# Converting double-precision weights beside attention: from three-step pieces to a pipeline over slots

## The chip, the cores and the metric

The kernel runs on one core of a Trainium2 chip. The core has five engines with a queue of instructions each: TensorE (PE, with its weight loads as PEld), VectorE (DVE), ScalarE (ACT), GpSimd (POOL) and SyncE (SP), which here only issues DMAs. Each engine runs its queue in program order, and semaphores join the queues. The metric is the device time of one launch in microseconds; the profile comes from one separate profiled execution.

## What is computed

The reference first runs an attention with a threshold over 8 batches, 8 heads, 576 tokens and a head dimension of 64, in float32. A score that lies more than tau below its row's maximum is dropped before the softmax. The 8 heads of a token are joined to 512 features, and a mixer follows:

```python
scores = scale * np.matmul(q, k.transpose(0, 1, 3, 2))
thresh = np.max(scores, axis=-1, keepdims=True) - tau
scores = np.where(scores >= thresh, scores, -1000000000.0)
attn = softmax(scores); x = heads_joined(np.matmul(attn, v))
h = np.maximum(xt @ w_tok1, 0.0) @ w_tok2      # xt: features x tokens
u = x + h.transpose(0, 2, 1)
out = u + np.maximum(u @ w_ch1, 0.0) @ w_ch2
```

The four weights (576x256, 256x576, 512x1536, 1536x512) arrive as 64-bit floats. The kernel turns them into 32-bit floats itself, with integer and float operations on the two 32-bit words of each number.

## The kernel before

**Attention.** The work goes in 144 units, 18 per batch; a unit is 128 query rows of two heads. In the main loop (from L513) a unit does its scores on TensorE (`scores`, L286), the row maxima on VectorE (L291) and a small bias on GpSimd (L292). Then `weigh` puts the threshold (L301) and the exponential (L304) on ScalarE. One unit later `norm` divides by the row sum (reciprocal on VectorE, L310 and L311; scaling on GpSimd, L314). Two units later the weights are transposed. In batch 0 TensorE does it and VectorE or ScalarE copies the result (`turn`, L337 and L339). In later batches VectorE transposes blocks (`turn_blocks`, L348), and 16 DMAs on SP's queue move the blocks (L358), for every second unit and for the shared one. `values` multiplies with v (L388, L393) and ScalarE copies to xT (L398). The scores lie in PSUM in two double-bank buffers, three in batch 0, so new scores wait until ScalarE has read the old ones at L301.

**MLP.** When a batch's attention is complete, `push` puts its mixer steps into a list: transposes of x (L412, L413), the token products (L422, L429, with VectorE adding the result to xT at L433), and the channel products (L451 with ScalarE's ReLU at L452; L463 and L467 with the copy at L472 and a DMA out). `fill` takes steps from the list in three portions of each unit, 0.4, 0.3 and 0.3 of a quota worked out from written costs. So TensorE's order is the program's, and batch 0 has no MLP steps. They begin in unit 20, once batch 0 is complete. The products share two PSUM buffers.

**Weights.** There are 31 pieces: three of w_tok1, four of w_tok2 (288 columns), 12 of w_ch1, 12 of w_ch2, most of 128 x 512 numbers. `load_piece` (L187, its DMA on SP at L196) brings a piece into one of three raw buffers in a scratch tile. `f64_to_f32` (L145) has six instructions:

- ScalarE L159: the low words, scaled by 2^-29, in place
- ScalarE L160: the square of the high words read as floats, into the one buffer h2
- VectorE L161 and L164: shift and mask the exponent's and the fraction's bits, into one of two buffers a; put the sign back
- VectorE L167: zero for numbers that are too small, by h2
- GpSimd L168: the integer add of a and the low words, into the weight tile

The generator yields after L161, after L164, and after L168 with the load of the piece three further on. One yield is a step, so three steps make a piece. `weight(n)` (L216) takes n steps at two places in the loop: at L544, before `weigh`, and at L556, at the end of the unit. n is 1 and 1 in batch 0, then 4 and 3. `need(i)` (L224) takes the steps that piece i still lacks before a matmul reads it.

Of the kernel before, what the change touches and what calls it, by code (L numbers as in the profile page):

```python
# [9 lines left out]
F32 = mybir.dt.float32  # L10
U32 = mybir.dt.uint32
I32 = mybir.dt.int32
I64 = mybir.dt.int64
AF = mybir.ActivationFunctionType
ALU = mybir.AluOpType
AX = mybir.AxisListType

P = 128
# [3 lines left out]
def kernel(  # L22
# [26 lines left out]
    nc = tc.nc  # L49
# [21 lines left out]
    work = ctx.enter_context(tc.tile_pool(name="work", bufs=2))  # L71
# [38 lines left out]
    def load_v(n):  # L110

        b, p = pairs[n]
        lv = ld.tile([P, NK, D], F32, tag="lv", bufs=4, name=f"lv_{n}")
        nc.sync.dma_start(out=lv, in_=v[b].rearrange("h s d -> (h s) d")[2 * S * p : 2 * S * p + 2 * S, :].rearrange("(c p) d -> p c d", p=P))
        vals[n] = lv
# [15 lines left out]

    WMAX = 512
    scratch = work.tile([P, NP * 2 * S], U32, tag="xT", name="scratch")
    NRAW = 3
    raw_at = [scratch[:, 2 * WMAX * i : 2 * WMAX * (i + 1)] for i in range(NRAW)]
    a_at = [scratch[:, 2 * WMAX * NRAW + WMAX * i : 2 * WMAX * NRAW + WMAX * (i + 1)] for i in range(2)]
    sq_at = scratch[:, 2 * WMAX * NRAW + 2 * WMAX : 2 * WMAX * NRAW + 3 * WMAX].bitcast(F32)
    turn_of = [0]

    def like(x, dst):  # L140
        if len(dst.shape) == 2:
            return x
        return x.rearrange("p (a b) -> p a b", a=dst.shape[1])

    def f64_to_f32(dst, raw, rows, n):  # L145

        lo, hi = raw[:, :, 0], raw[:, :, 1]
        a = a_at[turn_of[0] % 2][0:rows, 0:n]
        h2 = sq_at[0:rows, 0:n]
        turn_of[0] += 1
        af = a.bitcast(F32)
        nc.scalar.activation(out=lo.bitcast(I32), in_=lo, func=AF.Copy, scale=2.0**-29)  # L159
        nc.scalar.activation(out=h2, in_=hi.bitcast(F32), func=AF.Square)  # L160
        yield nc.vector.tensor_scalar(  # L161
            out=a, in0=hi, scalar1=3, scalar2=0x3FFFFFFF, op0=ALU.logical_shift_left, op1=ALU.bitwise_and
        )
        yield nc.vector.scalar_tensor_tensor(  # L164
            out=a, in0=hi, scalar=0xC0000000, in1=a, op0=ALU.bitwise_and, op1=ALU.bitwise_or
        )
        nc.vector.scalar_tensor_tensor(out=af, in0=h2, scalar=2.0**-30, in1=af, op0=ALU.is_ge, op1=ALU.mult)  # L167
        nc.gpsimd.tensor_tensor(  # L168
            out=dst.bitcast(I32), in0=like(a.bitcast(I32), dst), in1=like(lo.bitcast(I32), dst), op=ALU.add
        )  # L170

    pieces = [
        (w1[:, 2 * i : 2 * i + 2, :], moe_w_tok1[2 * P * i : 2 * P * i + 2 * P, :].rearrange("(t p) x -> p t x", p=P))
        for i in range(NI // 2)
    ]
# [6 lines left out]
    for j in range(NJ):  # L182
        pieces.append((wc2[:, j, :], moe_w_ch2[P * j : P * j + P, :]))

    raws = {}

    def load_piece(i):  # L187
        dst, src = pieces[i]
        rows = dst.shape[0]
        n = 1  # L190
        for d in dst.shape[1:]:
            n *= d
        wide = src.dtype == I64
        raw = raw_at[i % NRAW][0:rows, 0 : n * (2 if wide else 1)]
        raw = raw.bitcast(src.dtype)
        nc.sync.dma_start(out=like(raw, dst), in_=src)  # L196
        raws[i] = raw, rows, n

    def weight_ops():
        for i, (dst, src) in enumerate(pieces):  # L200
            raw, rows, n = raws.pop(i)
            if src.dtype == I64:
                for _ in f64_to_f32(dst, raw.bitcast(U32).rearrange("p (n w) -> p n w", w=2), rows, n):
                    yield
            else:
                yield
                yield
                nc.gpsimd.tensor_copy(out=dst, in_=like(raw, dst))
            if i + NRAW < len(pieces):
                load_piece(i + NRAW)  # L210
            yield

    wops = weight_ops()
    steps_done = 0

    def weight(n):  # L216

        nonlocal steps_done
        for _ in range(n):
            if next(wops, wops) is wops:  # L220
                return
            steps_done += 1

    def need(i):  # L224

        weight(3 * i + 3 - steps_done)

    load_piece(0)
    load_qk(1, (nc.sync, nc.sync))
# [1 line left out]
    for i in range(1, NRAW):  # L231
        load_piece(i)
    load_v(1)

# [23 lines left out]
    def in_blocks(b):  # L260
        return b > 0
# [10 lines left out]
    def scores(u):  # L272
        b, p0, t = units[u]
        sc = [
            (ps_3rd if b == 0 and (2 * u + h) % 3 == 2 else ps_sc).tile([P, 2, MAIN], F32, tag="sc", name=f"sc{h}_{u}") for h in range(2)
        ]
        if t == SHARED:
            parts = [(b * NP + p0 + i, slice(MAIN, S), slice(64 * i, 64 * i + 64)) for i in range(2)]
        else:
            i, c = divmod(t - (t > SHARED), NI)  # L280
            parts = [(b * NP + p0 + i, slice(P * c, P * c + P), slice(0, P))]
        order = [(f, part, h) for f in range(2) for part in parts for h in range(2)]
        for f, (n, cols, rows), h in order if b else sorted(order, key=lambda o: o[2]):
            r = slice(D * h, D * h + D)
            qT, kT = heads[n]
            nc.tensor.matmul(sc[h][rows, f, 0:HS], lhsT=qT[r, cols], rhs=kT[r, HS * f : HS * f + HS], start=True, stop=True)  # L286
        mx = small.tile([P, 2], F32, tag="mx", name=f"mx_{u}")
        bias = small.tile([P, 2], F32, tag="bias", name=f"bias_{u}")
        for h in range(2):
            c = slice(h, h + 1)  # L290
            nc.vector.tensor_reduce(out=mx[:, c], in_=sc[h][:, :, 0:HS], axis=AX.XY, op=ALU.max)  # L291
            nc.gpsimd.tensor_scalar(out=bias[:, c], in0=mx[:, c], scalar1=toff, scalar2=-SCALE, op0=ALU.add, op1=ALU.mult)  # L292
        st[u] = sc, bias
# [13 lines left out]
    def norm(u):  # L307
        e, rs = st[u]
        rr = small.tile([P, 2], F32, tag="rr", name=f"rr_{u}")
        nc.vector.tensor_scalar(out=rr, in0=rs, scalar1=1e-9, scalar2=None, op0=ALU.add)  # L310
        nc.vector.reciprocal(out=rr, in_=rr)  # L311
        for h in range(2):
            eh = e[:, S * h : S * h + S]
            nc.gpsimd.tensor_scalar(out=eh, in0=eh, scalar1=rr[:, h : h + 1], scalar2=1.0, op0=ALU.mult, op1=ALU.mult)  # L314
        st[u] = e
# [195 lines left out]
    b_now = 0  # L511
    LAG = 2
    for u in range(len(units) + LAG + 4):  # L513
        on = u < len(units)
        if u == UB:
            late.close()
            ps_mm = ctx.enter_context(tc.tile_pool(name="ps_mm", bufs=2, space=bass.MemoryType.PSUM))
        if on:
            b_now, p0, t = units[u]
            n = b_now * NP + p0  # L520
        w = u - LAG
        back = 0 <= w < len(units)
        if on:
            scores(u)
        if 0 < u <= len(units):
            norm(u - 1)
        if back:
            key, place, many = group_of(w)
            if in_blocks(key[0]):
                turn_blocks(w)  # L530
            else:
                for i in range(3):
                    turn(w, i)
            if place == many - 1:
                b, p, c = key
                if c == 0 and p % 2 == 0:
                    split_middle(b * NP + p)
                if c == "s":
                    split_middle(b * NP + p + 1)
                when = u + (2 if in_blocks(b) else 1)  # L540
                due += [(when, b, p + i, c) for i in range(2 if c == "s" else 1)]
        if b_now:
            fill(0.4)
        weight(4 if b_now else 1)  # L544
        if on:
            weigh(u)
        if b_now:
            fill(0.3)
        while due and due[0][0] <= u:
            _, b, p, c = due.popleft()  # L550
            values(b, p, c)
            if p == NP - 1 and c == 1:
                push(b)
        if b_now:
            fill(0.3)
        weight(3 if b_now else 1)  # L556
        if on:
            m = n + 2 + t // 4
            if t < 8 and m < len(pairs):
                load_qk(m, (nc.scalar if b_now else nc.sync,) * 2, t % 4)  # L560
                if t % 4 == 3:
                    load_v(m)
            if t == 2:
                prep(n + 1)
            if t == 7 and n + 2 < len(pairs):
                prep(n + 2)
    weight(10000)
    quota = 1e9
    fill(1.0)
# [28 lines left out]
```

## Time and profile before

| | |
|---|---|
| median of three runs | 1420.17 us (1418.49 to 1422.05) |
| profiled execution | 1421.9 us span, 1424.03 us device time, mean granted TensorE clock 0.984 |
| TensorE busy | 1346.7 us, 95% |
| its weight loads | 832.4 us, 59% |
| VectorE busy | 584.1 us, 41% |
| ScalarE busy | 589.8 us, 41% |
| GpSimd busy | 345.4 us, 24% |
| first and last L168 | 18.9 us, 201.1 us |

The shares are means over the whole span. The page's slices cut the span into 40 parts of 35.5 us, with a digit for each engine's busy tenths and a line for the clock that TensorE was granted. The windows view gives busy time for any stretch. The waits view says in one line which instruction stood idle, what released it, how long in total, how often, and the longest. The groups view lists instructions of one kind: busy time, mean ns of one, then the idle time before them and what ended it. The timeline lists instructions in order: start, length, queue, line. The chain of waits goes back from the last instruction to what released each step.

### The profile page before, as it was taken

Reading aid. Unit: us, or ns where it says so; the run is one execution under the profiler, and the core shown is the slowest. Engines: PE = TensorE matmul, PEld = TensorE weight load, DVE = VectorE, ACT = ScalarE, POOL = GpSimd, SP = SyncE. Lnnn points to the kernel's source line nnn. Section 1 sums busy time; section 2 is a strip of 40 time slices with the busy share of each in tenths; the row PEclk is TensorE's granted clock in tenths of the full one; section 3 lists DMA queues with packets and bytes.
Section 4 is the critical chain, followed back from the end, with each engine's and each line's share of the span. In section 5 each row is a group of like instructions: output and inputs, shape, how many; then the busy total and the mean of one; then the engine's idle time right before and its main releaser. Section 6 shows DMA issues by size and latency. Waiting matters only on the chain.

```text
span 1421.9 us, 19495 instructions
## 1 busy us (share of the span) xinstructions
PE 1346.7 (95%) x6866; PEld 832.4 (59%) x6866; DVE 584.1 (41%) x1009; ACT 589.8 (41%) x1328; POOL 345.4 (24%) x681
## 2 busy tenths in 40 slices
PE   6777689988999999999999999999999999999998
PEld 4443455645656566565656566566657466566675
DVE  5888654344344443434433444334333443201000
ACT  5776353443545444353434444353334344220110
POOL 4565332222222222222212222222121222100000
PEclk9998899989999999999999999999999999999999
DMA  6344544443444434443343534443433433300000
GB/s 130 90 117 131 152 125 103 92 116 84 102 120 111 108 84 106 104 98 80 92 101 77 121 80 111 104 98 69 103 87 83 111 91 78 82 15 15 8 8 23
DMA packets 257376, 128.34 MB, mean 90 GB/s; under 512 B 208064, under 2 KB 221376, under 8 KB 257280
## 3 DMA queue, kind: packets, MB, share of 16 engines
q1 hardware_dynamic: 131632, 111.46, 29.9%
q10 hardware_dynamic: 125648, 15.64, 6.9%
q8 instruction: 55, 0.90, 0.3%
q14 instruction: 41, 0.34, 0.1%
HBM read 43.25 MB, written 9.44 MB: 37 GB/s over the span
## 4 chain that ended last, share of the span: by engine, by line
PE 81%; DVE 8%; SPq 5%; DMA 3%; ACT 3%; issue 1%; POOL 0%; DVEq 0%; ACTq 0%
PE c L467 26%; PE c L451 24%; PE sc L286 10%; PE pv L393 7%; SPq L358 5%; PE t L422 3%; PE t L429 3%; DVE mx L291 3%; PE pv L388 2%; DVE T L348 2%; PE tx L412 2%; PE c L463 1%; DMA eT<-T 1%; DMA scratch<-in_moe_w_ch_dram 1%; ACT e L301 1%
## 5 line engine op out<-in xcount | busy, mean ns | idle before, releaser
L451 PE MATMUL c<-xT,wc 128*128 128x256 f32 (+1 forms) x1920 | 406.2, 363 | 1.9 <-DVE xT L433 0.8
L291 DVE TENSOR_REDUCE mx<-sc 128x1 f32<-128x576 f32 x288 | 204.6, 751 | 489.5 <-PE sc L286 489.4
L467 PE MATMUL c<-wc,g 128*128 128x512 f32 x864 | 389.5, 597 | 0.0
L451 PEld LDWEIGHTS c<-xT,wc 128*128 128x128 f32 x1920 | 331.7, 190 | 75.9 <-issue 29.9
L292 POOL TENSOR_SCALAR bias<-mx,toff 128x1 f32<-128x1 f32 x288 | 76.7, 267 | 807.8 <-DVE mx L291 754.1
L301 ACT ACTIVATE e<-sc,bias 128x576 f32<-128x576 f32 x288 | 199.2, 741 | 169.7 <-POOL bias L292 148.8
L467 PEld LDWEIGHTS c<-wc,g 128*128 128x128 f32 x864 | 157.6, 190 | 177.3 <-issue 175.9
L452 ACT ACTIVATE g<-c 128x256 f32<-128x256 f32 (+1 forms) x240 | 87.3, 364 | 386.0 <-PE c L451 366.5
L304 ACT ACTIVATE e<-e,ntau 128x576 f32<-128x576 f32 x288 | 220.8, 774 | 0.0
L314 POOL TENSOR_SCALAR e<-e,rr 128x576 f32<-128x576 f32 x288 | 213.4, 753 | 17.3 <-DVE rr L311 4.1
L286 PE MATMUL sc<-kT,qT 64*128 64x288 f32 (+1 forms) x1280 | 196.7, 441 | 20.0 <-ACT e L301 10.9
L348 DVE STREAM_TRANSPOSE T<-e 128x1152 f32<-128x1152 f32 x126 | 172.5, 1369 | 16.5 <-DMA eT<-T 10.8
L286 PEld LDWEIGHTS sc<-kT,qT 64*128 64x128 f32 (+1 forms) x1280 | 107.1, 181 | 102.1 <-issue 50.1
L393 PE MATMUL pv<-eT,lv 128*64 128x256 f32 x1024 | 124.0, 385 | 0.0
L472 DVE COPY o<-c 128x512 f32<-128x512 f32 x36 | 24.6, 684 | 192.7 <-PE c L467 192.7
L393 PEld LDWEIGHTS pv<-eT,lv 128*64 128x64 f32 x1024 | 75.7, 140 | 38.0 <-issue 2.6
L429 PE MATMUL t<-w,a 128*128 128x288 f32 x256 | 78.8, 437 | 17.8 <-DVE xT L433 15.8
L422 PE MATMUL t<-x,w 128*128 128x512 f32 (+1 forms) x160 | 76.0, 613 | 0.0
L429 PEld LDWEIGHTS t<-w,a 128*128 128x128 f32 x256 | 46.7, 197 | 42.6 <-DVE xT L433 20.8
L398 ACT COPY xT<-pv 128x256 f32<-128x256 f32 x64 | 23.9, 373 | 107.4 <-PE pv L393 107.3
L433 DVE TENSOR_TENSOR xT<-xT,t 128x288 f32<-128x288 f32 x64 | 27.9, 442 | 96.5 <-PE t L429 96.4
L304 ACT ACTIVATION_READ_ACCUMULATOR e<-e,ntau 128x1 f32 x288 | 57.4, 199 | 0.0
(43 smaller groups left out, 600.4 us busy)
## 6 DMA issues: line engine op xcount, KB each, us to landing
eT<-T SPq DMA_DIRECT2D x896, 72.0 KB, 2.0
scratch<-in_moe_w_ch_dram SPq DMA_DIRECT2D x24, 512.0 KB, 3.8
lv<-in_v_dram SPq DMA_DIRECT2D x32, 288.0 KB, 3.3
out_dram<-o SPq DMA_DIRECT2D x36, 256.0 KB, 2.2
eT<-T SPq DMA_DIRECT2D x224, 36.0 KB, 1.9
lk<-in_k_dram ACTq DMA_DIRECT2D x108, 72.0 KB, 2.7
lq<-in_q_dram ACTq DMA_DIRECT2D x104, 72.0 KB, 2.1
lq<-in_q_dram SPq DMA_DIRECT2D x24, 72.0 KB, 3.3
```

The source lines that it names most:

```text
L286: nc.tensor.matmul(sc[h][rows, f, 0:HS], lhsT=qT[r, cols], rhs=kT[r, HS * f : HS * f + HS], start=True, stop=True)
L291: nc.vector.tensor_reduce(out=mx[:, c], in_=sc[h][:, :, 0:HS], axis=AX.XY, op=ALU.max)
L301: nc.scalar.activation(out=eh, in_=sc[h][:, :, 0:HS], func=AF.Prelu, bias=bias[:, h : h + 1], scale=SCALE, alpha=STEEP)
L304: nc.scalar.activation(out=eh, in_=eh, func=AF.Exp, bias=ntau, accum_out=rs[:, h : h + 1])
L314: nc.gpsimd.tensor_scalar(out=eh, in0=eh, scalar1=rr[:, h : h + 1], scalar2=1.0, op0=ALU.mult, op1=ALU.mult)
L348: nc.vector.transpose(out=T.rearrange("p (a c n x) -> p c a n x", a=4, c=NK, n=n)[:, :, :, place, :], in_=e.rearrange("p (c a x) -> p c a ...
L393: nc.tensor.matmul(to[r], lhsT=lv[:, j, :], rhs=eT[:, j], start=False, stop=(c == NI - 1), skip_group_check=True)
L422: nc.tensor.matmul(ps, lhsT=w1[0:M, t, P * m : P * m + P], rhs=s["x"][0:M, t, :], start=(t == 0), stop=(t == NT - 1))
L429: nc.tensor.matmul(ps, lhsT=s["a"][:, m, P * c : P * c + P], rhs=w2[:, m, HS * f : HS * f + HS], start=(m == 0), stop=(m == NTK - 1))
L451: nc.tensor.matmul(ps, lhsT=wc1[:, j, c, :], rhs=uT[:, c, GR * i : GR * i + n], start=(c == 0), stop=(c == NCC - 1))
L452: nc.scalar.activation(out=s["g"][:, j, 0:n], in_=ps, func=AF.Relu)
L467: nc.tensor.matmul(flat, lhsT=s["g"][:, j, P * t : P * t + P], rhs=wc2[:, j, :], start=False, stop=(j == NJ - 1), skip_group_check=True)
```

## The change

The generator of steps is replaced by a counter of slots. In one slot GpSimd adds the piece of the slot before, ScalarE does its two operations for the piece of the slot after, VectorE does its three for the slot's own piece in a row, and the load of the piece three further than the slot's is issued on SP behind GpSimd's add. VectorE writes into the weight tile itself, and GpSimd adds in place. The raw buffers become four. The square h2 takes the two buffers of the output tile (tag "o"). ScalarE's part of piece 0 comes ahead of the main loop.

The places move too. In batch 0 there is one slot at the end of each unit but every fourth (u % 4 = 3). In later batches there is one slot right after `norm`, ahead of `turn_blocks` and its DMAs, and one at the end of the unit. `need(i)` takes slots until slot i + 1 is done.

```diff
-    NRAW = 3
+    NRAW = 4
...
+            h2 = work.tile([P, WMAX], F32, tag="o", name=f"h2_{i}")[0:rows, 0:n]
...
+    def on_scalar(i):
+        if i < len(pieces) and pieces[i][1].dtype == I64:
+            lo, hi, h2 = raws[i]
+            nc.scalar.activation(out=lo.bitcast(I32), in_=lo, func=AF.Copy, scale=2.0**-29)
+            nc.scalar.activation(out=h2, in_=hi.bitcast(F32), func=AF.Square)
...
+    def on_vector(i):
...
+            nc.vector.tensor_scalar(
+                out=bits, in0=hi, scalar1=3, scalar2=0x3FFFFFFF, op0=ALU.logical_shift_left, op1=ALU.bitwise_and
+            )
+            nc.vector.scalar_tensor_tensor(
+                out=bits, in0=hi, scalar=0xC0000000, in1=bits, op0=ALU.bitwise_and, op1=ALU.bitwise_or
+            )
+            nc.vector.scalar_tensor_tensor(out=dst, in0=h2, scalar=2.0**-30, in1=dst, op0=ALU.is_ge, op1=ALU.mult)
...
+    def weight():
+        nonlocal slot
+        if slot <= len(pieces):
+            on_gpsimd(slot - 1)
+            on_scalar(slot + 1)
+            on_vector(slot)
+            if slot:
+                load_piece(slot - 1 + NRAW)
+            slot += 1
...
     def need(i):
...
-        weight(3 * i + 3 - steps_done)
+        while slot < i + 2:
+            weight()
...
+    on_scalar(0)
...
             norm(u - 1)
+        if b_now:
+            weight()
         if back:
...
-        weight(4 if b_now else 1)
         if on:
             weigh(u)
...
-        weight(3 if b_now else 1)
+        if b_now or u % 4 < 3:
+            weight()
```

More of the change, by code (lines that the diff above doesn't have):

```diff
@@ L133 @@
     scratch = work.tile([P, NP * 2 * S], U32, tag="xT", name="scratch")
-    NRAW = 3
+    NRAW = 4
     raw_at = [scratch[:, 2 * WMAX * i : 2 * WMAX * (i + 1)] for i in range(NRAW)]
-    a_at = [scratch[:, 2 * WMAX * NRAW + WMAX * i : 2 * WMAX * NRAW + WMAX * (i + 1)] for i in range(2)]
-    sq_at = scratch[:, 2 * WMAX * NRAW + 2 * WMAX : 2 * WMAX * NRAW + 3 * WMAX].bitcast(F32)
-    turn_of = [0]
     def like(x, dst):
@@ L143, in like @@
         return x.rearrange("p (a b) -> p a b", a=dst.shape[1])
[L145 to L170, printed above, removed]
     pieces = [
@@ L187, in load_piece @@
     def load_piece(i):
+        if i >= len(pieces):
+            return
         dst, src = pieces[i]
@@ L193, in load_piece @@
         wide = src.dtype == I64
-        raw = raw_at[i % NRAW][0:rows, 0 : n * (2 if wide else 1)]
-        raw = raw.bitcast(src.dtype)
+        raw = raw_at[i % NRAW][0:rows, 0 : n * (2 if wide else 1)].bitcast(src.dtype)
         nc.sync.dma_start(out=like(raw, dst), in_=src)
[L197 to L201, printed above, removed]
+        if wide:
+            words = raw.bitcast(U32).rearrange("p (n w) -> p n w", w=2)
+            h2 = work.tile([P, WMAX], F32, tag="o", name=f"h2_{i}")[0:rows, 0:n]
+            raws[i] = like(words[:, :, 0], dst), like(words[:, :, 1], dst), like(h2, dst)
+        else:
+            raws[i] = like(raw, dst)
@@ new lines, in on_scalar @@
+    def on_scalar(i):
[4 more added lines that the diff above has]
+    def on_vector(i):
+        if i < len(pieces) and pieces[i][1].dtype == I64:
+            dst = pieces[i][0]
+            lo, hi, h2 = raws[i]
+            bits = dst.bitcast(U32)
+            nc.vector.tensor_scalar(
[5 more added lines that the diff above has]
+            nc.vector.scalar_tensor_tensor(out=dst, in0=h2, scalar=2.0**-30, in1=dst, op0=ALU.is_ge, op1=ALU.mult)
@@ L202, in weight_ops, with on_gpsimd @@
+    def on_gpsimd(i):
+        if 0 <= i < len(pieces):
+            dst, src = pieces[i]
             if src.dtype == I64:
-                for _ in f64_to_f32(dst, raw.bitcast(U32).rearrange("p (n w) -> p n w", w=2), rows, n):
-                    yield
-            else:
[L206 to L222, printed above, removed]
+                nc.gpsimd.tensor_tensor(out=dst.bitcast(I32), in0=dst.bitcast(I32), in1=raws.pop(i)[0].bitcast(I32), op=ALU.add)
+            else:
+                nc.gpsimd.tensor_copy(out=dst, in_=raws.pop(i))
+    slot = 0
+    def weight():
[7 more added lines that the diff above has]
+            slot += 1
@@ L566 @@
                 prep(n + 2)
-    weight(10000)
+    need(len(pieces) - 1)
     quota = 1e9
```

## The prediction

> **What bounds it now.** I read first the page's slices, then busy time by stage, then TensorE's waits in the stage with holes. The slices (each 35.5 us):
>
> ```profile
> PE   6777689988999999999999999999999999999998
> DVE  5888654344344443434433444334333443201000
> ...
> PEclk9998899989999999999999999999999999999999
> ```
>
> TensorE has holes in the first six slices and small ones near the ninth. Later it is full: the kernel is bound by TensorE, except where the weights are converted. The scores' start times in the timeline give the unit borders: unit 3 starts at 21.75 us, 18 (batch 1) at 98.18, 20 at 115.44, 27 at 205.86. Busy time by these stages:
>
> ```profile
> 21.75:98.18 76.43, 59.30 (x472) 38.22 (x471) 62.44 (x135) 58.08 (x128) 44.29 (x77) 1.00 0.42 97
> 98.18:115.44 17.26, 10.13 (x56) 5.78 (x55) 15.14 (x28) 11.10 (x24) 11.22 (x14) 0.82 0.55 150
> 115.44:205.86 90.42, 70.26 (x333) 45.12 (x333) 62.56 (x94) 48.34 (x100) 37.00 (x49) 0.86 0.50 138
> ...
> 432.33:1280.00 847.67, 842.25 (x4353) 518.25 (x4353) 326.64 (x551) 347.70 (x798) 187.18 (x398) 1.00 0.38 91
> ```
>
> Columns: window, length, then busy us of TensorE, its weight loads, VectorE, ScalarE, GpSimd, then granted clock, DMA share, GB/s. In batch 0 VectorE is busy 82% (62.44 of 76.43). Units 18 and 19 have no MLP steps yet, and VectorE is busy 88%. Units 20 to 26 have MLP steps, and there TensorE is busy 70.26 of 90.42 us, at a clock of 0.86. From 432 to 1280 us it is idle 5.4 of 848. Its order and work don't change there, so what is saved before 206 us should reach the end whole. What TensorE waits for from 98 to 206 us (total, times, longest):
>
> ```profile
> PE t L429 <- DVE xT L433: 11.1, 2, 8.0
> PE sc L286 <- ACT e L301: 7.6, 4, 3.4
> PE tx L412 <- ACT xT L398: 4.7, 1, 4.7
> PE tr L337 <- DVE eT L339: 3.1, 2, 2.2
> ```
>
> None names the conversion, but what stands in front of these instructions on VectorE and ScalarE does. All engines' waits in the same window:
>
> ```profile
> ACT scratch L160 <- DVE scratch L167: 16.7, 6, 4.5
> ACT scratch L159 <- DMA scratch<-in_moe_w_ch_dram: 14.6, 4, 7.1
> DVE scratch L161 <- DMA scratch<-in_moe_w_ch_dram: 9.5, 3, 4.3
> DVE scratch L167 <- ACT scratch L160: 7.8, 2, 4.3
> ```
>
> Queues keep program order. While ScalarE stands at L160 or L159, the weighing behind it (L301) stands too, and the next scores wait for its PSUM. While VectorE stands at L161, the additions at L433 stand, and the token product L429 waits for PSUM. The longest, 8.0 us, is shown by the chain: a load is issued at 146.98 us behind 16 block moves on SP, lands 4.06 us later, and then come L161, L164, L433. SP's timeline and the costs of one conversion in the stage:
>
> ```profile
> 136.82 10.06 SPq L358 DMA_DIRECT2D eT<-T  x16
> 146.98 1.02 SPq L196 DMA_DIRECT2D scratch<-in_moe_w_ch_dram  x2
> ...
> L164 DVE SCALAR_TENSOR_TENSOR scratch<-scratch 128x512 uint32<-128x512 uint32 x20 | 23.9, 1196 | 0.5
> L167 DVE SCALAR_TENSOR_TENSOR scratch<-scratch 128x512 f32<-128x512 f32 x20 | 14.4, 720 | 10.0 <-ACT scratch L160 7.8 <-ACT e L304 0.5 <-DVE scratch L164 0.5
> L161 DVE TENSOR_SCALAR scratch<-scratch 128x512 uint32<-128x512 uint32 x19 | 8.9, 469 | 9.5 <-DMA scratch<-in_moe_w_ch_dram 9.5
> ```
>
> **What the skill says.** The Trainium skill, "SBUF — State Buffer", section "Who interferes with whom": a VectorE instruction with two SBUF inputs contends with a GpSimd instruction that reads SBUF. The trace agrees: L164 has both inputs in SBUF and takes 0.68 us at its fastest, 1.66 where it starts 0.3 us behind GpSimd's L168 (1.40). "TensorE: Matmul & The Clock Gate", section "The HAM clock gate (the 'warmup' mystery)": an idle TensorE has its clock halved until it is busy again. The trace agrees: 0.82 and 0.86 in the stages with holes, 1.00 after 432 us. "DMA: Bandwidth & Descriptors", section "Issuing engines are not separate DMA queues", calls the issue time usually small. Here the trace differs: 16 issues hold SP for 10.06 us, 0.63 each, against 2.0 us from issue to landing.
>
> **The change, part by part.**
>
> Same arithmetic. One piece on VectorE costs 0.42 + 0.69 + 0.69 = 1.80 us uncontended (fastest 0.414, 0.682, 0.675), 0.47 + 1.20 + 0.72 = 2.39 by the stage's means. Writing in place and moving h2 to the output tile's buffers change neither counts nor sizes: nothing, since output tiles are first written after the last conversion. Three-dimensional views on VectorE and ScalarE (14 pieces) I take as free too; were L161 as slow there as L164 alone (0.69, 0.27 more), that is 3.8 us.
>
> Pace. In batch 0 it was 2 of 3 steps per unit, 36 steps, 12 pieces in 18 units; now 14 slots (every unit except u%4 = 3). In batch 1 it was 7 steps per unit, 19 pieces; now two slots per unit, slots 14 to 31, which hold VectorE pieces 14 to 30, 17 of them. Both end in unit 26. need() forces neither: the first use of the channel weights comes after 2.2 + 8.6 + 7.8 = 18.6 us of planned token steps at 6 us per unit (103 planned us over 17 units).
>
> Batch 0. Two more pieces on VectorE cost 2 x 1.80 to 2 x 2.39, 3.6 to 4.8 us. Where a values product (2.3 us of TensorE) stands before the next scores, VectorE has room and they hide; elsewhere they show. I take +2. Three steps in one block before the next maximum instead of two is the bigger unknown: bounds -3 (the skipped unit gains and the first loads are one earlier) and +24 (rival D). The fourth load before the start adds one SP issue, 0.4 us, behind the first unit's loads: hidden, scores start at 9.04 us whatever it does.
>
> Units 18 and 19. Per unit VectorE: maxima 2 x 0.744, reciprocal 0.33, copies 1.9, two pieces 4.8: 8.5, for two units 17.0 against 17.26 measured. Nothing gained.
>
> Units 20 to 26. VectorE needs per unit: maxima 1.49, reciprocal 0.33, block transpose 1.36, additions 8 x 0.444 / 7 = 0.51, preparation 3.0 / 7 = 0.43, together 4.1, and two pieces 3.6 to 4.8: 7.7 to 8.9. TensorE's work at full clock: 70.26 less 0.14 of the clock times 90.42 us times its busy share 0.78, 9.8, gives 60.4, or 8.6 per unit. So both are nearly equal, and TensorE can't go below 60.4. What I leave on top of it:
> - L429 <- L433: 8.0 of it was a load that VectorE waited for; now VectorE touches a piece one slot after ScalarE saw it landed, so this wait goes. But the first slot now stands before the block transpose, so the additions stand behind maxima 1.49, reciprocal 0.33, piece 2.39 and transpose 1.36, 5.6 us, while TensorE brings two token steps (2.2 us) and the scores (1.2). I keep 2 waits of 3.5 (5.6 less 2.2): 7.
> - L286 <- L301, 7.6: ScalarE no longer waits for L167 (16.7 us of waits). I keep 2. The 4.7 at L412 goes, its ScalarE copy stood behind the same waits.
> - Loads: the first slot's load is now ahead of the 16 block moves and the second's behind them. Queued behind a waiting load on SP are exactly those moves; the load waits for GpSimd's add of the piece before, 0.75 x 2 + 1.3 us after the reciprocal, less than the piece and transpose (3.8) that the moves wait for anyway: free. SP has four groups in units 21 to 26 (40 us) and 2 loads per unit (about 1). Where groups follow in neighbouring units (23, 24) the second slot's load comes some 17 us after the unit's start, and lands 4 later; ScalarE wants it 14 after. That stands ScalarE 0 to 7 us, of which I let 2 reach TensorE.
> - Clock: 9.8 lost before, I keep 3 for a third of the idle time.
>
> Sum 60.4 + 7 + 2 + 2 + 3 = 74.4 against 90.4: -16. With batch 0's +2 the net is -14: 1421.9 to 1408 in the profiled execution, which is 1.7 above the median of 1420.17. So 1406 us.
>
> **Rivals.**
>
> B: down to TensorE's own limit. If L433's waits hide behind other steps and loads are always in time, units 20 to 26 take 62 and batch 0 nothing: -28, 1392. For: VectorE's 7.7 to 8.9 fits in 8.6. Against: the first slot stands ahead of transpose and additions.
>
> C: the loads stay late. Two slots per unit, 16 moves between, SP 41 of 60 us full: if ScalarE stands as long for loads as now (14.6) and half of that reaches TensorE with its clock, -5, 1415. For: the longest wait of the stage is such a load. Against: the fourth buffer gives each load a slot more. That ScalarE isn't ahead in fact is here too: with two h2 buffers its piece needs L167 of two pieces before, a slot earlier, so it should be.
>
> D: slower. In batch 0 three steps in a block stand directly before the next maximum, and GpSimd's add, no longer waiting for L167, runs beside them. At the longest durations seen (1.02 + 1.67 + 0.99 = 3.67) the 11 blocks of units 3 to 17 cost 40 us against 16.6 there now (VectorE's busy time on the scratch tile alone, in that window): +24, less 16 gives +8, 1428. It decides above (16.6 + 16) / 11 = 3.0 us a block, all of it exposed. Against: the units with values products have room, and the longest durations came beside adds only.
>
> **The numbers.** Likeliest case 0.45 (1406), B 0.20 (1392), C 0.22 (1415), D 0.13 (1428). About 0.3%, 4.3 us, is what a measurement tells from no change, so faster means below 1416: the first two and half of C, 0.76; same 0.12; slower 0.12. The range goes from just under B to part of D's way, 1391 to 1419.
>
> **What would show it.** Right: ScalarE's square no longer waits for VectorE's last operation on the piece before, and VectorE waits for no load; unit 20 to 27 takes 75 us, unit 3 to 18 about 78; everything after shifts whole. Wrong: waits for the weight load on ScalarE over 10 us (C); blocks of over 3 us and a batch 0 over 85 us (D); TensorE idle in units 20 to 26 below 4 us (B). If the stages shorten and the end does not, the whole shift was wrong.

## The result and the profile after

The changed kernel takes 1426.35 us (median of four runs, 1424.96 to 1428.98) against 1419.33 before (four runs). The ratio is 1.0049, 95% interval 1.0028 to 1.0069. A second set of runs gives 1.0037 (1.0023 to 1.0051). So it is slower by about 7 us, where 14 us faster was forecast. Only the MLP stage of batch 1 came near its forecast.

In the changed kernel ScalarE's operations are L184 and L185, VectorE's L192, L195 and L198, GpSimd's add L204, the load L173; from L285 on the old lines stand one lower. The slices of the changed kernel's page answer to those shown of before:

```profile
PE   6676799978999999999999999999999999999998
...
DVE  6878674344444443434433444434333444201000
```

TensorE's fourth to sixth slices, 7, 6, 8 before, are 6, 7, 9 now. VectorE's first four, 5 8 8 8 before, are 6 8 7 8. This is too coarse to see a loss. The windows are sharper. Their borders are the starts of the first row maximum of units 3, 18, 20 and 27, which I use as markers from here on (the prediction's borders were starts of scores). The windows view of the changed kernel, columns as in the prediction:

```profile
25.80:114.40 88.60, 62.01 (x471) 38.81 (x471) 71.35 (x138) 60.82 (x130) 47.07 (x79) 0.94 0.40 94
114.40:133.50 19.10, 11.15 (x56) 6.28 (x58) 15.26 (x26) 10.54 (x21) 11.55 (x12) 0.74 0.44 126
133.50:208.10 74.60, 63.29 (x327) 40.71 (x324) 56.29 (x87) 42.48 (x90) 42.67 (x46) 0.93 0.51 141
```

The same borders give this table for both kernels, each profiled twice:

| us | start of unit 3 | 3 to 18 | 18 to 20 | 20 to 27 | 27 to 36 | 36 to 45 | rest | span |
|---|---|---|---|---|---|---|---|---|
| before | 25.1 | 75.6 | 18.2 | 88.3 | 79.4 | 74.7 | 1060.7 | 1421.9 |
| before, again | 24.6 | 76.7 | 18.2 | 86.8 | 79.4 | 73.0 | 1060.4 | 1419.0 |
| changed | 25.8 | 88.6 | 19.2 | 74.6 | 79.4 | 76.5 | 1060.7 | 1424.7 |
| changed, again | 27.1 | 91.8 | 19.1 | 73.9 | 79.4 | 75.1 | 1060.6 | 1427.0 |

The MLP stage of batch 1 (units 20 to 27) gains 13 to 14 us. Batch 0 (units 3 to 18) loses 13 to 15. By the prediction's borders the first profile of the changed kernel has +10.5 us in batch 0 (87.0 for 76.4), +3.9 in units 18 and 19 (21.2 for 17.3) and -13.5 in units 20 to 26 (76.9 for 90.4): the borders move 2 to 3 us of the loss from one stage into the next.

After unit 27 everything shifts whole, but for units 36 to 45. That stage lies between 72.3 and 76.5 in all fourteen profiles, with the same order of work in each, and it goes with the granted clock: seven profiles at 0.93 take 72.3 to 73.0, four at 0.91 take 74.4 to 75.1, three at 0.89 take 76.1 to 76.5. In the first pair it adds 1.8 us to the difference. So a difference of 2 us between two profiles says nothing without the clock beside it. The spans of the two pairs differ by 2.8 and 8.0 us, while the medians of the runs differ by 7.

The loss is clearest from unit 10 to 18. Those eight units take 51.0 to 51.3 us in each of four profiles of kernels that run the changed kernel's batch 0. With the batch 0 of before they take 40.3 in two profiles and 42.0 in a third (e8), where one unit ran in part at half clock. The windows of these eight units hold TensorE's share of it. First the kernel before:

```profile
60.33:100.66 40.33, 30.02 (x250) 19.52 (x250) 34.52 (x72) 32.19 (x68) 25.42 (x41) 1.00 0.42 102
```

Then the changed kernel:

```profile
63.08:114.40 51.32, 33.78 (x250) 20.99 (x249) 41.04 (x75) 33.90 (x71) 27.36 (x42) 0.93 0.40 97
```

With the same 250 matrix products TensorE is busy 3.8 us longer, as its clock falls from 1.00 to 0.93, and idle 7.2 us longer (17.5 against 10.3). VectorE is busy 6.5 us longer. The timeline of the changed kernel shows how. Unit 10 holds no values product and a block; unit 11 holds a values product and no block:

```profile
65.76 1.25 PE L285 MATMUL sc<-kT,qT 64*128 64x288 f32 x8
...
66.35 0.42 DVE L192 TENSOR_SCALAR wc<-scratch 128x512 uint32<-128x512 uint32 x1
66.40 1.52 POOL L204 TENSOR_TENSOR wc<-wc,scratch 128x512 int32<-128x512 int32 x1
66.80 1.67 DVE L195 SCALAR_TENSOR_TENSOR wc<-scratch,wc 128x512 uint32<-128x512 uint32 x1
68.58 0.69 DVE L198 SCALAR_TENSOR_TENSOR wc<-h,wc 128x512 f32<-128x512 f32 x1
69.18 1.41 DVE L290 TENSOR_REDUCE mx<-sc 128x1 f32<-128x576 f32 x2
70.79 1.00 DVE L338 COPY eT<-tr 128x384 f32<-128x384 f32 x2
...
71.38 0.65 PE L387 MATMUL pv<-eT,vl 128*64 128x256 f32 x4 [2.14 <-DVE eT L338]
71.86 3.16 PE L392 MATMUL pv<-eT,lv 128*64 128x256 f32 x16
...
74.95 1.62 PE L285 MATMUL sc<-kT,qT 64*128 64x288 f32 x8
...
76.67 1.42 DVE L290 TENSOR_REDUCE mx<-sc 128x1 f32<-128x576 f32 x2 [3.54 <-PE sc L285]
```

The scores of unit 11 ended at 67.01, but their maximum stands behind the whole block (2.8 us) and starts 2.2 us later. GpSimd's add starts 0.05 us behind the block's first operation, and L195 takes 1.67 us in place of 0.69. TensorE waits 2.14 us for the copies behind the maximum. Then its clock is halved, as the windows view shows:

```profile
73.40:75.10 1.70, 1.70 (x10) 0.64 (x6) 0.00 (x0) 0.04 (x1) 0.00 (x0) 0.50 0.00 0
```

The values product takes 3.16 us where the same one took 1.90 before. VectorE has no block to do in that time and waits 3.54 us.

### The profile page after: what moved, and what is told of

Its sections match the earlier page's. It is cut to its first block, busy times and chain, and to the rows that moved or that the text cites. A ratio compares the mean times of both kernels' runs of the same rounds, so it can differ in the third digit from the quotient of the medians.

```text
span 1424.7 us, 19491 instructions
## 1 busy us (share of the span) xinstructions
PE 1346.6 (95%) x6866; PEld 830.6 (58%) x6866; DVE 591.9 (42%) x1009; ACT 588.0 (41%) x1328; POOL 356.2 (25%) x681
## 4 chain that ended last, share of the span: by engine, by line
PE 80%; DVE 8%; SPq 5%; ACT 2%; DMA 2%; issue 1%; POOL 1%; ACTq 0%; DVEq 0%
PE c L466 26%; PE c L450 23%; PE sc L285 10%; PE pv L392 7%; SPq L357 5%; PE t L421 4%; PE t L428 3%; PE pv L387 3%; DVE mx L290 2%; DVE T L347 1%; PE c L462 1%; PE tx L411 1%; DMA eT<-T 1%; ACT e L300 1%; DVE eT L338 1%
## 5 line engine op out<-in xcount | busy, mean ns | idle before, releaser
L451 ACT ACTIVATE g<-c 128x256 f32<-128x256 f32 (+1 forms) x240 | 86.8, 362 | 383.4 <-PE c L450 361.8
L313 POOL TENSOR_SCALAR e<-e,rr 128x576 f32<-128x576 f32 x288 | 219.8, 776 | 17.1 <-DVE rr L310 4.3
L285 PE MATMUL sc<-kT,qT 64*128 64x288 f32 (+1 forms) x1280 | 194.5, 438 | 14.7 <-DVE kT L267 7.9
L285 PEld LDWEIGHTS sc<-kT,qT 64*128 64x128 f32 (+1 forms) x1280 | 105.7, 181 | 97.0 <-issue 51.8
L392 PE MATMUL pv<-eT,lv 128*64 128x256 f32 x1024 | 128.8, 396 | 0.0
L471 DVE COPY o<-c 128x512 f32<-128x512 f32 x36 | 24.6, 684 | 192.3 <-PE c L466 192.3
L392 PEld LDWEIGHTS pv<-eT,lv 128*64 128x64 f32 x1024 | 78.0, 144 | 40.5 <-issue 6.7
L428 PEld LDWEIGHTS t<-w,a 128*128 128x128 f32 x256 | 46.7, 196 | 38.7 <-DVE xT L432 17.3
L432 DVE TENSOR_TENSOR xT<-xT,t 128x288 f32<-128x288 f32 x64 | 27.9, 440 | 98.9 <-PE t L428 98.9
```

The lines of the kernel that those rows point to most:

```text
L392: nc.tensor.matmul(to[r], lhsT=lv[:, j, :], rhs=eT[:, j], start=False, stop=(c == NI - 1), skip_group_check=True)
L428: nc.tensor.matmul(ps, lhsT=s["a"][:, m, P * c : P * c + P], rhs=w2[:, m, HS * f : HS * f + HS], start=(m == 0), stop=(m == NTK - 1))
L451: nc.scalar.activation(out=s["g"][:, j, 0:n], in_=ps, func=AF.Relu)
```

## The experiments

All stages are in us, in the markers of the table above. "3-10" and "10-18" divide batch 0.

| | ratio to before (95%) | 3-10 | 10-18 | 18-20 | 20-27 |
|---|---|---|---|---|---|
| before | | 35.3 | 40.3 | 18.2 | 88.3 |
| changed | 1.0049 (1.0028 to 1.0069) | 37.3 | 51.3 | 19.2 | 74.6 |
| e1 other units | 1.0015 (1.0003 to 1.0026) | 40.8 | 44.0 | 19.0 | 73.9 |
| e2 add in its own slot | 0.9931 (0.9909 to 0.9953) | 36.4 | 44.1 | 18.8 | 74.8 |
| e3 three steps in batch 0 | 0.9972 (0.9959 to 0.9985) | 38.1 | 40.5 | 18.9 | 76.0 |
| e4 slot behind the moves | 1.0088 (1.0056 to 1.0120) | 39.1 | 51.0 | 18.1 | 83.6 |
| e5 e1 and e2 | 0.9956 (0.9943 to 0.9970) | 42.4 | 41.1 | 17.8 | 73.8 |
| e6 e3, add behind its piece | 0.9966 (0.9953 to 0.9979) | 36.5 | 40.5 | 17.7 | 74.9 |
| e7 three load buffers | 1.0109 (1.0086 to 1.0131) | 39.0 | 51.3 | 19.1 | 86.4 |
| e8 before, steps ahead of moves | 0.9969 (0.9955 to 0.9982) | 34.7 | 42.0 | 20.4 | 81.6 |
| e9 13 slots, add in its own slot | 0.9936 (0.9913 to 0.9959) | 36.5 | 41.1 | 19.1 | 73.3 |
| e10 e6 with a late first step | 0.9946 (0.9929 to 0.9963) | 36.5 | 40.5 | 17.9 | 75.4 |

The starts of the maxima also give the length of each single unit (us). V marks a unit with a values product, b one in which the kernel converts a block:

| | 10 | 11 V | 12 | 13 V | 14 | 15 V | 16 V | 17 |
|---|---|---|---|---|---|---|---|---|
| before (single operations) | 3.97 | 5.96 | 4.28 | 5.87 | 4.66 | 5.78 | 5.55 | 4.25 |
| changed | 6.10 b | 7.49 | 5.06 b | 5.95 b | 6.10 b | 7.54 | 7.38 b | 5.69 b |
| e1 | 4.02 | 7.07 b | 3.94 | 5.95 b | 4.02 | 5.86 b | 7.45 b | 5.67 b |
| e2 | 5.12 b | 5.84 | 5.05 b | 5.98 b | 5.12 b | 5.85 | 6.41 b | 4.77 b |
| e9 | 4.02 | 6.10 b | 3.95 | 5.95 b | 4.02 | 5.85 b | 6.48 b | 4.77 b |

Before converts five pieces of 512 in these units, the changed kernel and e2 six, e1 and e9 five.

**e1: the slots at other units.** Two theories of batch 0's loss stood against each other. One was the units at which the blocks stand, the other was GpSimd's add beside them.

```diff
-        if b_now or u % 4 < 3:
+        if b_now or u in (0, 1, 2, 3, 4, 5, 6, 7, 9, 11, 13, 15, 16, 17):
```

> The changed kernel with its 14 slots of batch 0 at other units: 0 to 7, 9, 11, 13, 15, 16, 17, so that all eight units that hold a values product have a block and only two units without one past unit 4 do. Place theory (blocks stand bare where VectorE limits, and the units with values, where TensorE limits, hide none): units 3 to 18 fall from 87.0 us to 76 to 80, the whole to about 1417. Contention theory (GpSimd's add now runs beside the block in the same slot): blocks stay as long as they are and units 3 to 18 stay at 84 to 88, the whole at 1424 to 1427. Quantity theory (two more pieces in batch 0): the same, 84 to 88.

The place theory's forecast failed: units 3 to 18 took 84.8 us and the whole 1424.56, as the contention and the quantity theory had it. The stage hides two opposite effects. Past unit 10 the place mattered, 44.0 for 51.3, though one piece fewer is converted there. Ahead of it the edit lost 3.5 us against the changed kernel's first profile (40.8 for 37.3; its second had 40.6, with TensorE longer at half clock). It put more blocks there: unit 3 took 4.18 us with a block for 2.48 without, unit 7 6.60 for 4.86.

**e2: the add in its own slot.**

```diff
-            on_gpsimd(slot - 1)
             on_scalar(slot + 1)
             on_vector(slot)
+            on_gpsimd(slot)
```

> The changed kernel with GpSimd's add of a piece in the piece's own slot, behind VectorE's three operations, in place of one slot later. Then the add waits for VectorE and runs beside the next maximum or block transpose. Contention theory: VectorE's block falls from about 2.9 to 1.9 us, units 3 to 18 from 87.0 us to 77 to 80, units 20 to 27 from 76.9 by another 3 to 6, the whole to 1412 to 1416. Place theory: blocks get shorter, but units 3 to 18 still take over 82 us, the whole 1420 to 1424. If the one-slot lag of the add helps, as it was meant to, this gets slower than 1426.

The contention theory held in the main for batch 0 (80.6 us, just above its 77 to 80) and for the whole, 1412.36 us. Of the 14.1 us between the two profiles 8.0 lie in batch 0; 4.2 lie in units 36 to 45, which the edit does not touch. It did not hold for units 20 to 27, which stayed at 74.8. The groups view shows what the edit did to the blocks of batch 0. First VectorE of the kernel before in units 3 to 18, for the pieces of 128 x 512 (count, busy us and mean ns, then idle time before):

```profile
L164 DVE SCALAR_TENSOR_TENSOR scratch<-scratch 128x512 uint32<-128x512 uint32 x5 | 4.4, 872 | 0.1
L167 DVE SCALAR_TENSOR_TENSOR scratch<-scratch 128x512 f32<-128x512 f32 x5 | 3.4, 688 | 0.7 <-ACT e L304 0.5
L161 DVE TENSOR_SCALAR scratch<-scratch 128x512 uint32<-128x512 uint32 x5 | 2.1, 421 | 0.0
```

Then the changed kernel's:

```profile
L195 DVE SCALAR_TENSOR_TENSOR wc<-scratch,wc 128x512 uint32<-128x512 uint32 x7 | 9.0, 1292 | 0.2
L198 DVE SCALAR_TENSOR_TENSOR wc<-h,wc 128x512 f32<-128x512 f32 x7 | 7.1, 1010 | 0.6
L192 DVE TENSOR_SCALAR wc<-scratch 128x512 uint32<-128x512 uint32 x7 | 2.9, 419 | 0.0
```

Then e2's, same view, same units:

```profile
L195 DVE SCALAR_TENSOR_TENSOR wc<-scratch,wc 128x512 uint32<-128x512 uint32 x7 | 6.1, 874 | 0.2
L198 DVE SCALAR_TENSOR_TENSOR wc<-h,wc 128x512 f32<-128x512 f32 x7 | 4.8, 692 | 0.6
L192 DVE TENSOR_SCALAR wc<-scratch 128x512 uint32<-128x512 uint32 x7 | 2.9, 417 | 0.0
```

A block falls from 2.72 us to 1.98, the latter being what before had (0.421 + 0.872 + 0.688). In e2's timeline the add now runs beside the row maximum, and the maximum keeps its 1.41 us:

```profile
64.42 0.69 DVE L195 SCALAR_TENSOR_TENSOR wc<-scratch,wc 128x512 uint32<-128x512 uint32 x1
65.21 0.69 DVE L198 SCALAR_TENSOR_TENSOR wc<-h,wc 128x512 f32<-128x512 f32 x1
65.82 1.41 DVE L290 TENSOR_REDUCE mx<-sc 128x1 f32<-128x576 f32 x2
65.99 1.29 POOL L204 TENSOR_TENSOR wc<-wc,scratch 128x512 int32<-128x512 int32 x1 [1.93 <-DVE wc L198]
```

The clock of units 10 to 18 is 1.00 again. So the wait that the one-slot lag was there to avoid did no harm on GpSimd, and the lag itself cost VectorE 0.74 us a block. Unit by unit, units 10, 14, 16 and 17 with a block are 0.9 to 1.0 us shorter in e2 than in the changed kernel. Units 11 and 15, which have no block in either, are 1.7 us shorter: the changed kernel's TensorE spent 3.4 us of each at half clock. These six make the 7.2 us.

**e3: three steps in batch 0.** The slots are cut into steps again: `on_vector` now yields after L192 and after L195. Batch 0 has 12 slots as before, and batch 1 keeps its two whole slots.

```diff
-            on_vector(slot)
...
+            for _ in on_vector(slot):
+                yield
+            yield
...
+        if not b_now:
+            weight(1)
         if on:
             weigh(u)
...
-        if b_now or u % 4 < 3:
-            weight()
+        weight(3 if b_now else 1)
```

> The changed kernel with its slots cut into three steps again, and in batch 0 the old places and pace: one step before the weighing and one at the unit's end, so 12 slots in batch 0; in batch 1 the two whole slots per unit stay where they are (20 slots, one unit longer). Place and quantity theories: units 3 to 18 go back to 76 to 79 us, units 20 to 27 stay at 76 to 79, the whole 1411 to 1416, below both kernels. Contention theory: adds still run beside L192 to L198, so units 3 to 18 stay above 82, the whole above 1421.

Units 3 to 18 took 78.7 us, as the place and quantity theories had it, and units 10 to 18 took 40.5, like before. But this does not speak against contention, for the add hardly met the operations here: for pieces of 512 they took 0.420 + 0.775 + 0.841 = 2.04 us on average, as long as in e6, where the add has no lag. The steps took away the block, the meeting with the add and two pieces at once. The whole was 1417.71 us, above the forecast: unit 3 started only at 28.9 us.

**e4: the first slot behind the block moves.**

```diff
-        if b_now:
-            weight()
         if back:
...
         if b_now:
+            weight()
             fill(0.4)
```

> The changed kernel with the first slot of each unit of batch 1 behind the transposes (turn, turn_blocks) in place of ahead of them. If the slot ahead of the copies is what made units 18 and 19 longer (TensorE waited up to 6.0 us for a copy there), 18 to 20 fall from 21.2 us to 16 to 18. If the slot ahead of the 16 block moves is what gave units 20 to 27 their gain (loads in time), these go from 76.9 up to 85 or more, and the whole to 1430; if they owe it to ScalarE and VectorE no longer waiting for each other, they stay at 75 to 79 and the whole falls to 1421 to 1424.

Units 20 to 27 went from 74.6 to 83.6 us, a little under the forecast of 85: two thirds of their gain is the slot's place. The edit puts the slot's work on ScalarE and VectorE behind the transposes together with its load, so the order on SP is not parted from the order on these two. Units 18 and 19 took 18.1 us for 19.2. That is no more than the difference between e2 and e5 (18.8 and 17.8), whose program is the same there. SP's timeline shows the difference. In the changed kernel one load stands behind a group of 16 moves; its neighbours were issued ahead of the group:

```profile
149.38 10.06 SPq L357 DMA_DIRECT2D eT<-T  x16
159.56 0.51 SPq L173 DMA_DIRECT2D scratch<-in_moe_w_ch_dram  x1
```

In e4 two stand there:

```profile
147.60 10.05 SPq L357 DMA_DIRECT2D eT<-T  x16
157.76 1.01 SPq L173 DMA_DIRECT2D scratch<-in_moe_w_ch_dram  x2
```

**e5: both cures of batch 0 (e1 and e2).**

> Both edits together: the add in the piece's own slot and the 14 slots at the other units. From the first maximum of unit 3 to that of unit 18 before took 75.6 us, the change 88.6, units alone 84.8, the add alone 80.5. If the two causes are separate (place 4, contention 8), this gives 76 to 78 us, units 20 to 27 stay at 74 to 76, the whole at 1407 to 1411. If they are one (a contended block is what stands bare), it stays at 80 to 81 and the whole at 1411 to 1413.

Units 3 to 18 took 83.5 us: a miss of both forecasts, and 2.9 more than e2 alone. It is parted by unit 10. From 10 to 18 it is 41.1, so both cures together take 10.2 of the 11.0 us that were lost there. Each alone takes 7.2 or 7.3. They are not separate: a block in unit 15 costs nothing even when it is contended (5.86 in e1, 5.85 without one in e2), and a block without contention costs less where it is bare. From 3 to 10 the edit of e1 cost 6.0 us against e2. The blocks in units 3 and 7 are 3.0 of this (4.18 for 2.48, 6.17 for 4.86). So over the whole of batch 0 the other units are no cure.

**e6: three steps, with the add behind its own piece.** e3, with the add emitted behind L198.

> Three steps with the old places and pace in batch 0 (78.7 us there), and in addition the add behind L198 of its own piece. If contention is all that still parts it from before (75.6), batch 0 falls to 75 to 77 and the whole from 1417.7 to 1408 to 1413, since batch 1's slots gain by the uncontended blocks too. If the rest is the two whole slots' own start-up (earlier loads, ScalarE one piece ahead), batch 0 stays at 78 to 79 and the whole at 1414 to 1417.

Units 3 to 18 took 77.0 us, within the forecast. The whole was 1416.41, which the other theory had. The start explains it: unit 3 begins at 28.6 us. e6's timeline of ScalarE:

```profile
15.03 0.65 ACT L184 ACTIVATE scratch<-scratch 128x512 int32<-128x512 uint32 x1 [5.75 <-DMA scratch<-in_moe_w_tok_dram]
```

Being one piece ahead, ScalarE asks for the second piece in front of the first weighing, and stands 5.75 us for its load.

**e7: three load buffers.**

```diff
-    NRAW = 4
+    NRAW = 3
```

> The changed kernel with three load buffers. A load is then issued one slot later for its piece. If the fourth buffer carries the gain of units 20 to 27 (74.6 us), they go to 82 or more and the whole to 1434 or more, with ScalarE's waits for loads from 14.7 to over 22 us. If the order on SP (load ahead of the 16 moves) and the lack of a ring between ScalarE and VectorE carry it, they stay at 74 to 78 and the whole at 1424 to 1429. Batch 0 stays within 2 us of 88.6 in both.

Units 20 to 27 take 86.4 us, nearly as long as before. ScalarE's waits for loads there, first the changed kernel, then e7:

```profile
ACT scratch L184 <- DMA scratch<-in_moe_w_ch_dram: 14.7, 5, 4.9
```

```profile
ACT scratch L184 <- DMA scratch<-in_moe_w_ch_dram: 25.8, 6, 8.9
```

In this pipeline the fourth buffer is worth 11.8 us: without it each load is issued one slot later, and ScalarE, one piece ahead, stands for it. No run gives the kernel before a fourth buffer, so what it is worth alone is not known.

**e8: before, with its first four steps ahead of the transposes and moves.**

```diff
+        if b_now:
+            weight(4)
         if back:
...
-        weight(4 if b_now else 1)
+        if not b_now:
+            weight(1)
```

> The kernel before with one thing of the change alone: in batch 1 its four steps stand ahead of the transposes and block moves, not behind. If the place of the loads ahead of the moves is what the change gained by (the slot behind them cost 9 us), units 20 to 27 fall from 88.3 to 78 to 81 and the whole from 1420 to 1410 to 1413. If the ring of ScalarE and VectorE over the one h2 buffer, and the wait of both on the same load, are what held it, they stay at 85 to 90 and the whole at 1417 to 1422. Batch 0 stays at 75.6.

Between the two: 81.6 us, 6.7 less than before, with 2.2 given back in units 18 and 19. Its waits in units 20 to 27 show both causes side by side, the load and the ring over the one h2 buffer:

```profile
ACT scratch L159 <- DMA scratch<-in_moe_w_ch_dram: 11.3, 5, 5.3
ACT scratch L160 <- DVE scratch L167: 11.1, 6, 4.3
```

So the early place alone gives half of the 13.7 us, and the pipeline over slots with its fourth buffer adds the other half.

**e9: thirteen slots.** e2, with slots at units 0, 1, 2, 4, 5, 6, 8, 9, 11, 13, 15, 16, 17.

> The add in its own slot, and past unit 9 the slots at the units with values (11, 13, 15, 16) and at 17 alone; units 0 to 9 as the change has them (0, 1, 2, 4, 5, 6, 8, 9). That is 13 slots in batch 0, one fewer. From the maximum of unit 10 to that of 18 the change took 51.3 us, before 40.4, the add alone 44.1, add and other units together 41.2. If a block at a unit with values is free once it isn't contended, units 10 to 18 take 40.5 to 42, units 3 to 10 stay at the 36.6 of the add alone, and the whole is 1408 to 1411. If what the other units gained there came from the blocks they moved ahead of unit 10, units 10 to 18 stay at 43 to 45 and the whole at 1412 to 1414.

Units 10 to 18 took 41.1 us and 3 to 10 36.5, both as forecast, so place does matter past unit 10 and not through the moved blocks. It is one piece fewer too, but the unit lengths part place from number. Against e2, units 10, 12 and 14 are 1.10 us shorter each without their block. With a block unit 11 is 0.26 longer and unit 15 not at all. The whole, 1414.48 us, was above the forecast. Units 36 to 45 took 76.1 in its profile, 3.8 more than in e2's, and its six runs spread from 1408.40 to 1417.24. e9 can't be told from e2.

**e10: the first step later.** e6, with both steps of unit 0 at its end.

> Three steps with the add behind L198, as in the run with steps and the add in place, but unit 0 takes both its steps at its end. There ScalarE stood 5.75 us for the second piece's load ahead of the first weighing, and unit 3 began at 28.6 us against 25.1 before. If that wait is what those kernels lost at the start, unit 3 begins at 24 to 25.5 us and the whole falls from 1416 to 1411 to 1413. If the start is held by something else, it stays at 27.5 or more and the whole at 1415 to 1417.

Unit 3 begins at 25.9 us, 2.7 earlier and 0.4 later than forecast, so the wait for the second load was most of what the stepped kernels lost at the start. The whole is 1414.15 us, 1 above the forecast.

**Both kernels once more.** Their stages are in the first table.

> The changed kernel itself once more, for the spread of the stages. Units 3 to 18 again 86 to 91 us, 20 to 27 again 73 to 76, so these differences belong to the program. Units 36 to 45 took 76.5 in its first profile and 72.3 to 76.3 in eight other kernels with the same program there: if that is the phase in which the clock is halved at unit 36, it can fall on either side here; if the change does something there, it is 76 again. The whole 1424 to 1429.

> The kernel before once more, for the same purpose. Units 3 to 18 74 to 78 us, 18 to 20 17 to 21, 20 to 27 85 to 90; units 36 to 45 anywhere from 72 to 77.

Units 20 to 27 repeat within 1.5 us in both kernels, 3 to 18 within 3.2. The changed kernel's 91.8 us lies 0.8 above what was forecast; units 4 and 9 alone are 1.6 us longer each than in its first profile. Units 36 to 45 fell to 75.1 and 73.0, so no effect of the change is shown there. The runs of the changed kernel spread from 1421.27 to 1430.67 us.

e2, e9 and e10 beat before by most, 0.5 to 0.7%; e3, e5, e6 and e8 beat it by 0.3 to 0.4%. The intervals of the first three overlap, and that of e5 reaches into them, so no best one is named.

## Why the prediction was wrong

**Where TensorE has holes, and the shift to the end: right.** All that was won or lost before unit 27 arrived at the end, but for about 2 us of spread in units 36 to 45.

**Units 20 to 27: right in sum.** -16 was forecast and -13 to -14 measured. Of the terms, TensorE's waits for the addition L432 (L433 before) were put at 7 us and came to 7.6:

```profile
PE t L428 <- DVE xT L432: 7.6, 2, 3.9
...
DVE wc L192 <- DMA scratch<-in_moe_w_ch_dram: 0.5, 1, 0.5
```

The wait for a load that stood in front of this addition went, as was said: VectorE waited 0.5 us for loads in this stage, 9.5 before. One term was wrong: ScalarE was to stand 0 to 7 us for loads, and it stood 14.7, as long as before (14.6), so C's sign, over 10 us, was there. Still the stage got faster. That VectorE and the additions no longer stand with ScalarE fits this, but no run tests it alone. The fourth buffer was named only in a sentence against rival C, and e7 shows that it carries 11.8 us.

**Units 18 and 19: open.** 0 was forecast. +1 is measured by the maxima and +3.9 by the prediction's borders.

**Batch 0: the step that failed.** "I take +2", for two more pieces on VectorE, with the three steps in one block as an unknown of -3 to +24. Measured was +13 to +15. So the sum priced two more pieces and put the block itself, where it stands and what runs beside it, at nothing. In units 10 to 18 the changed kernel converts six pieces of 512, at units 10, 12, 13, 14, 16 and 17, for five before, and loses 11.0 us. At the 1.10 us that a bare block without contention costs (e2 against e9), one more piece does not make that. Two things did:

- the places. The units left out past unit 4 (7, 11, 15) all hold a values product. In 11 and 15 a block costs 0 to 0.26 us (e9 against e2), but in 7 it costs 1.3 to 1.7 (e5 against e2, e1 against the changed kernel). Six of the blocks past unit 4 stand in units without one (5, 8, 10, 12, 14, 17), where the next maximum waits for them. The prediction said that blocks hide where a values product stands, and did not go through the fourteen slots to see which ones do. The places and the one piece more are what still parts e2 from before, 3.8 us.
- the lag of the add. The prediction used 1.80 to 2.39 us a piece, from rows where the add of a piece comes behind its L167. The changed order puts the add beside L195 and L198 in most blocks (not in unit 12's): 2.72 us on average. The Trainium skill's rule on two SBUF inputs ("SBUF — State Buffer", section "Who interferes with whom") was quoted, and only rival D held the change against it; the likeliest case did not. e2 agrees with the rule: add moved, 0.74 us a block gone, and 7.2 of the 11.0 us with it.

What came on top was not in the sum at all. TensorE's own waits grew, and its clock fell to 0.93 in units 10 to 18, with the same products 3.8 us longer. The prediction allowed for the clock in batch 1 only. The half clock came with the lag and the bare blocks together: in e1, which keeps the lag, and in e2, which keeps the places, these units have a clock of 1.00. In e2 units 11 and 15 take back 3.3 us.

**Rival D was the nearest.** It named the block in front of the maximum and the add beside it, and gave 1428 us. But its price, 3.67 us a block and all of it bare, is not what happened. The blocks took 2.72 us, below the 3.0 from which it said it would decide. The rest of the loss came by TensorE's waits and clock. D's +24 for batch 0 was 10 too much, so that its total came within 2 us is in part luck. B and C fell: the stage gained half of what B wanted, and 13 where C left 5.

**Still open.** Why unit 7 hides no block although it holds values products was not settled. The other 3 us that e5 lost ahead of unit 10 against e2 stand beside a clock of 0.84 from 25.9 to 68 us, but whether that is cause or effect wasn't tried. The split of the 11.0 us between waiting and clock is read from unit lengths, and no kernel holds the clock fixed.

## What to carry to other kernels

A step that is made into a block should be followed slot by slot: in which units does it stand, what follows it on its engine, and is there other work to hide it in that very unit. An average per unit hides this, and leaving out every fourth slot can leave out the ones that were free. A lag that removes a wait on an engine off the critical path can be worth nothing, and where the lagging instruction then runs beside one that it slows, it costs: here the wait was the better choice. Running one piece ahead needed a buffer more and an early place for the loads. Of the 13.7 us in units 20 to 27 the early place alone gave 6.7 (e8), the pipeline with four buffers in the late place 4.7 (e4), and the pipeline in the early place with three buffers only 1.9 (e7).

## What was not expected of the hardware

GpSimd's add lengthened L195 by up to 0.98 us (1.67 for 0.69), while the row maximum beside the same add kept its 1.41 us. In units 10 to 18 of the changed kernel TensorE had two gaps of 2.14 us, and each was followed by 3.4 us at half clock: a values product of 16 instructions took 3.16 us for 1.90. Before had no gap over 1.55 us there and a clock of 1.00. This is no rule, for e8's unit 15 had such a stretch without a long gap (7.47 us for 5.78). And one stage far from any edit (units 36 to 45) differs by up to 4.2 us between profiles, with a clock of 0.93, 0.91 or 0.89, which is as much as several of the edits tried here.
